# Decay tables doubled on both sides at once, V in bands by way of memory, G's third band from PSUM, v times sums also on GpSimd, a new order

## The chip, the cores and the metric

The kernel runs on one core of a Trainium2 chip. The metric is the device time of one execution in microseconds (us). The engines are PE (TensorE, matmul), DVE (VectorE), ACT (ScalarE), POOL (GpSimd) and SP (SyncE, which here only issues DMAs). Each engine works through its own queue in order and waits for others by semaphores. A change under about 0.2% (0.8 us) can't be told from none here.

## What is computed

```python
# r, k, v: (4, 8, 768, 48);  w, u: (8, 48)
for t in range(S):
    cur = einsum('bhd,bhe->bhde', u * k_t, v_t)
    y_t = einsum('bhd,bhde->bhe', r_t, state + cur)
    state = w * state + einsum('bhd,bhe->bhde', k_t, v_t)
x = y, heads side by side                  # (4, 768, 384)
h = x^T @ U @ V                            # U (768, 32), V (32, 768)
u = x + h^T
out = u + relu(u @ w_ch1) @ w_ch2          # w_ch1 (384, 1536), w_ch2 (1536, 384)
```

## The kernel before

**Attention in chunks.** The 768 steps of a batch are six chunks of 128, each with two halves of 64; a chunk's number n runs over all batches, so 0 to 5 are batch 0. A chunk loads k, r and v (tiles `ld`, `ldk`, `ldr`, `ldv`, L800). PE transposes k and r (L919, into `ptk` and `ptr`). DVE (or ACT and a table on one side) multiplies them by powers of the decay w, from the table `tabT`, into kT and rT (L928; L930 and L931 are copies for chunks that scale k otherwise). PE makes the scores of each half (L951, into `pab`), DVE masks them (L1092, `am`), POOL scales k by the transposed table (L851, L854, `ks`), PE makes the state's updates (L965), DVE adds them to the state S (L1131, L1133), ACT scales S by wm (L1141, `SW`). The diagonal is separate: dv = r * k (L866, POOL), times u (L879), summed per head into dg (L886, DVE), and v * dg, back into `dv` (L890 on ACT per head; L894 on DVE two heads at a time). PE then sums am against v (L988) and S and SW against rT (L992), and DVE adds dv (L1101) to get x.

**The front.** The six chunks of batch 0 come first and nearly alone (the code calls them front(n)). From each x PE makes a part of G = x^T U (L1207, into `wake`). G is split into a high part, a low part and the high part again (L1231, L1239, L1235: three bands of 32 rows in the tile `Gs`), so that one matmul of depth 96 with V in three bands (`V3`: high, high, low) gives x^T U V at full precision. V comes from memory as 128 rows of 192 elements; PE spreads it to three bands of 32 rows by 768 with eight matmuls against the constant `sel` (lines 725 to 740), ACT casts it (L737) and DVE takes the low part (L738). Then PE transposes x and adds V·G into `pu`, `pab` or `pav`, ACT and DVE split the sum into uTh (L1314) and uTl (L1315).

**The MLP.** u goes through w_ch1 and w_ch2 in tiles of 128 by 384 (all these matmuls go through a helper, L473, whose writes are called p). hr is the relu (L1395), hh and hl its high and low parts (L1396, L1397), the last sum is L1435, the store L1443. The weights arrive as 64-bit words (`raw_w`, 384 KB each, L655), are taken apart and joined on DVE and ACT (L677 to L698) and split into high and low parts w1s and w2s (L717, L718). U and V take the same way (`raw_u`, `raw_v`).

**What sets the order.** A planner in the kernel (class Plan) simulates queues, DMAs and PE's instruction fetch (`BLOCK`, `FETCH`, `fetched`) as the program is built, and writes each engine's operations in the order in which they got their turn; each operation has a key, from its place in the code or from the table `RANKS`, which names operations by number. Operations with `alt` go to the engine that would have them done first. Between 10 and 48 us of the planner's time (`PACED`) each DMA that SP issues also waits for an operation of DVE or ACT, so that loads don't run ahead. `at(t, ...)` gives a step its due time; `LATER` is that of V's conversion.

## Time and profile before

| | us |
|---|---|
| timed runs, median of 3 (lowest, highest) | 404.32 (404.26, 404.48) |
| the profiled execution | 405.71 |
| its span | 404.0 |
| PE busy | 391.5 |
| DVE, ACT, POOL busy | 272.9, 186.7, 67.7 |

The span is what the hardware profiler recorded of one execution, from the first instruction to the last. Busy time is without waits; PE's and DVE's idle stretches are what a reader looks for, and which engine or DMA ended each.

### The profile page before, as it was taken

The numbers are of one execution on the slowest core, as the hardware profiler recorded it, in microseconds if no ns is written. First come the engines' busy times: TensorE is split into PE (matmuls) and PEld (weight loads), VectorE is DVE, ScalarE is ACT, GpSimd is POOL, SyncE is SP. The second block draws the span as 40 slices with busy tenths as digits, with TensorE's granted clock in tenths as the row PEclk, the third lists the DMA queues.
The fourth block names the chain that finished last, engine by engine and source line by source line (L and its number), as shares of the span: only waits on it lengthen the run. The fifth ranks groups of instructions, "written<-read, shape, count | busy, mean of one in ns | idle before, by whom it ended". The sixth has DMA issues, their size and how long they took to land.

```text
span 404.0 us, 11959 instructions
## 1 busy us (share of the span) xinstructions
PE 391.5 (97%) x4916; PEld 373.5 (92%) x4916; DVE 272.9 (68%) x618; ACT 186.7 (46%) x451; POOL 67.7 (17%) x83
## 2 busy tenths in 40 slices
PE   8988999999999999999999999999999999999994
PEld 5776998999999999999999999999989999999994
DVE  7988979989988897748944789666855561222122
ACT  3686877789552533421523326322322443323330
POOL 2971001031643321200200123101200000000000
PEclk9999999999999999999999999999999999999999
DMA  9968698985565884675656857754307420001001
GB/s 143 176 156 200 121 265 165 250 239 116 111 129 104 190 175 98 104 130 124 132 75 119 157 118 144 123 89 116 87 3 129 107 60 0 0 2 58 2 0 66
DMA packets 195693, 46.27 MB, mean 115 GB/s; under 512 B 179374, under 2 KB 194096, under 8 KB 195632
## 3 DMA queue, kind: packets, MB, share of 16 engines
q1 hardware_dynamic: 194304, 44.85, 55.2%
q8 instruction: 40, 0.66, 0.6%
q10 hardware_dynamic: 1328, 0.59, 0.5%
q14 instruction: 21, 0.17, 0.1%
HBM read 37.16 MB, written 8.26 MB: 112 GB/s over the span
## 4 chain that ended last, share of the span: by engine, by line
PE 88%; DMA 3%; DVE 3%; ACT 2%; issue 1%; SPq 1%; POOL 0%; DVEq 0%; POOLq 0%
PE p L473 70%; PE pab L951 3%; PE pav L1006 2%; PE pav L1011 2%; DMA raw_w<-in_moe_w_ch_dram 2%; PE pab L965 2%; DMA ld<-in_r_dram 1%; PE pab L473 1%; PE pav L988 1%; PE wake L473 1%; PE pab L1207 1%; PE pav L992 1%; PE ptr L919 1%; PE ptk L919 1%; PE pab L919 1%
## 5 line engine op out<-in xcount | busy, mean ns | idle before, releaser
L473 PE MATMUL p<-uTh,w1s 128*128 128x384 f32 x576 | 148.1, 338 | 0.2 <-ACT hr L1395 0.2
L473 PE MATMUL p<-w2s,hh 128*128 128x384 f32 x576 | 128.8, 336 | 0.6 <-ACT hh L1396 0.6
L1395 ACT ACTIVATE hr<-p 128x384 f32<-128x384 f32 x96 | 47.3, 493 | 156.8 <-PE p L473 152.5
L1397 DVE TENSOR_TENSOR hl<-hr,hh 128x384 fp32r<-128x384 f32 x82 | 45.2, 554 | 89.2 <-ACT hh L1396 76.7
L473 PEld LDWEIGHTS p<-uTh,w1s 128*128 128x128 f32 x576 | 102.5, 188 | 2.0 <-ACT hr L1395 0.7
L473 PEld LDWEIGHTS p<-w2s,hh 128*128 128x128 f32 x576 | 102.0, 188 | 1.4 <-ACT hh L1396 0.9
L473 PE MATMUL p<-uTl,w1s 128*128 128x384 f32 x288 | 96.3, 335 | 0.0
L473 PE MATMUL p<-w2s,hl 128*128 128x384 f32 x288 | 79.2, 339 | 0.0
L473 PEld LDWEIGHTS p<-uTl,w1s 128*128 128x128 f32 x288 | 54.0, 188 | 0.0
L1396 ACT CAST hh<-hr 128x384 fp32r<-128x384 f32 x96 | 49.1, 513 | 9.3 <-PE p L473 7.0
L473 PEld LDWEIGHTS p<-w2s,hl 128*128 128x128 f32 x288 | 52.1, 188 | 0.7 <-DVE hl L1397 0.2
L1397 POOL TENSOR_TENSOR hl<-hr,hh 128x384 fp32r<-128x384 f32 x14 | 14.2, 1014 | 103.9 <-ACT hh L1396 36.2
L890 ACT ACTIVATE dv<-ldv,dg 128x48 f32<-128x48 f32 x92 | 22.1, 321 | 4.2 <-DVE dg L886 3.9
L1435 DVE TENSOR_TENSOR x<-p,x 128x384 f32<-128x384 f32 x33 | 17.3, 547 | 6.8 <-PE p L473 6.7
L1092 DVE TENSOR_TENSOR am<-pab,mask 128x256 f32<-128x256 f32 x48 | 18.8, 412 | 0.2 <-PE pab L951 0.2
L951 PEld LDWEIGHTS pab<-rT,kT 48*64 48x64 f32 x768 | 13.4, 134 | 5.0 <-issue 2.8
L1101 DVE TENSOR_TENSOR x<-pav,dv 128x384 f32<-128x384 f32 x23 | 12.6, 548 | 6.4 <-PE pav L1011 4.8
L951 PE MATMUL pab<-rT,kT 48*64 48x64 f32 x768 | 16.6, 224 | 0.0
L691 DVE SCALAR_TENSOR_TENSOR raw_w<-raw_w 128x384 int32<-128x384 int32 x24 | 13.1, 551 | 0.9 <-POOL w2s L718 0.6
L698 ACT ACTIVATE raw_w<-raw_w 128x384 f32<-128x384 f32 x24 | 13.3, 565 | 0.8 <-DMA raw_w<-in_moe_w_ch_dram 0.8
L886 DVE TENSOR_REDUCE dg<-dv 128x8 f32<-128x384 f32 x24 | 12.9, 540 | 0.1
L910 DVE STREAM_TRANSPOSE kT<-bl 128x256 f32<-128x256 f32 x30 | 12.4, 422 | 0.0
(190 smaller groups left out, 503.0 us busy)
## 6 DMA issues: line engine op xcount, KB each, us to landing
raw_w<-in_moe_w_ch_dram SPq DMA_DIRECT2D x24, 384.0 KB, 5.0
ldv<-in_v_dram SPq DMA_DIRECT2D x24, 192.0 KB, 4.2
ldk<-in_k_dram SPq DMA_DIRECT2D x20, 192.0 KB, 3.5
ldr<-in_r_dram SPq DMA_DIRECT2D x20, 192.0 KB, 3.1
bl<-in_r_dram SPq DMA_DIRECT2D x79, 48.0 KB, 2.7
bl<-in_k_dram SPq DMA_DIRECT2D x79, 48.0 KB, 2.4
ud<-x SPq DMA_DIRECT2D x18, 192.0 KB, 4.2
ub<-ud SPq DMA_DIRECT2D x18, 192.0 KB, 3.6
```

The source lines that it names most:

```text
L473: return nc.tensor.matmul(*args, **kw)
L691: return nc.vector.scalar_tensor_tensor(word(0), word(1), 3, word(0), ALU.logical_shift_left, ALU.bitwise_or)
L698: on_act(n, lambda: nc.scalar.activation(word(1).bitcast(F32), word(1).bitcast(F32), AF.Copy, scale=2.0 ** -112), [(raw, "hi")], loaded)
L886: on_dve(384, lambda e: e.tensor_reduce(dg.t, dv.t, AX.X, ALU.add), [dg], [dv])
L890: nc.scalar.activation(dv.t[:, h], v_of(n, h), AF.Copy, scale=dg.t[:, h:h + 1])
L951: return nc.tensor.matmul(pt.t[o * C2:(o + 1) * C2, q * C2:(q + 1) * C2], lhsT=kT.t[rows, q, i * C2:(i + 1) * C2], rhs=rT.t[rows, q, i * C ...
L1092: on_dve(256, lambda e: e.tensor_tensor(am.t, abs_[n][j].t[:, :SU].rearrange("p (h t) -> p h t", h=NP), mask_.unsqueeze(1).broadcast_to([1 ...
L1101: nc.vector.tensor_tensor(x.t[:, c0:c1], out_bank(n).t[:, c0:c1], dv.t.rearrange("p h d -> p (h d)")[:, c0:c1], ALU.add)
L1395: on_act(384, lambda: nc.scalar.activation(hr.t, pt.t[:, :TB], AF.Relu), [hr], [pt])
L1396: on_act(384, lambda: nc.scalar.copy(hh.t, hr.t), [hh], [hr])
L1397: on_either(384, lambda e: e.tensor_tensor(hl.t, hr.t, f32(hh.t), ALU.subtract), [hl], [hr, hh], only=None)
L1435: on_dve(384, lambda e, x=x, pt=pt: e.tensor_tensor(x.t, pt.t[:, :DM], x.t, ALU.add), [x], [pt])
```

## The change

1. `tables()` builds both sides of the decay table together: the clamped w is written to both, one reciprocal makes the other side, five doublings work on both at once, and the last doubling is done for one table and then for the other. The tile `inv`, two reciprocals, the outer product and two products go.
2. V's three bands are no longer made by PE. The tile `vh` gets the high part (ACT) and the low part (DVE) in the layout of memory, a DMA writes it to `vd` in DRAM, and three DMAs read it back as bands. `sel` and its copy go. `LATER` is 20.05 in place of 30.05.
3. G's third band is copied from PSUM, not from the first band. The rows of G are tracked apart (`G_ROWS`); the last chunk's x comes in two pieces, its product with U in three.
4. v * dg goes in fours of heads, on ACT, DVE or POOL. The first copy of S may go to ACT. Some pads are set by POOL.
5. The planner's constants for PE's instruction fetch are others, and so is the whole table `RANKS`, and with it the order on every engine. The last two stores have exchanged their queues.

```diff
-    BLOCK, FIRST = 126.5, 92
-    FETCH, BUSY, FETCHES = 1400, 1100, 48e3
+    FETCH, BUSY, FETCHES = 1600, 1100, 48e3
+    ASKED = 1500
...
-    sel = wbuf([128, 3 * 128], F32, "xh", NXS, "sel")
+    G_ROWS = [(wk, ("g", g)) for g in range(NCT)]
...
-        on_dve(4, lambda e: e.tensor_scalar(pw[:, 0, :, 1:2], pw_.t[:PD, :NP].unsqueeze(2), W_LO, W_HI, ALU.max, ALU.min),
-               [(tabT, 0)], [pw_])
+        on_dve(8, lambda e: e.tensor_scalar(at_(C2 + 1, (NP * W - 2, 2), (W, NP)),
+                                            pw_.t[:PD, :NP].unsqueeze(1).broadcast_to([PD, 2, NP]), W_LO, W_HI, ALU.max, ALU.min),
+               both, [pw_])
+        on_dve(32, lambda e: e.reciprocal(at_(C2 - 1, (NP * W + 2, 2), (W, NP)), at_(C2 + 1, (NP * W - 2, 2), (W, NP))), both, [])
+        def double(e, m, i, k):
+            o = i * NP * W
+            e.tensor_tensor(at_(o + C2 - 2 * m, (W, k * NP), (3 * m + 1, 2), (1, m)), at_(o + C2 - m, (W, k * NP), (m + 1, 2), (1, m)),
+                            at_(o + C2 - m, (W, k * NP), (2 * m, 2), (0, m)), ALU.mult)
         m = 1
-        while m < C2:
-            on_dve(4 * m, lambda e, m=m: e.tensor_mul(pw[:, 0, :, m + 1:2 * m + 1], pw[:, 0, :, 1:m + 1],
-                                                      pw[:, 0, :, m:m + 1].broadcast_to([PD, NP, m])), [(tabT, 0)], [])
+        while 2 * m < C2:
+            on_dve(16 * m, lambda e, m=m: double(e, m, 0, 2), both, [])
             m *= 2
-        on_dve(100, lambda e: e.reciprocal(inv.t[:, :, 0, 1:], pw[:, 0, :, 1:G8]), [inv], [(tabT, 0)])
-        on_dve(100, lambda e: e.reciprocal(inv.t[:, :, 1, 1:], pw[:, 0, :, G8:C2:G8]), [inv], [(tabT, 0)])
-        on_dve(28, lambda e: e.reciprocal(pw[:, 1, :, C2:], pw[:, 0, :, C2:]), [(tabT, 1)], [(tabT, 0)])
-        on_dve(256, lambda e: e.tensor_mul(pw[:, 1, :, :C2].rearrange("p q (a b) -> p q a b", b=G8),
...
         for x_ in (1, 0):
-            on_dve(256, lambda e, x_=x_: e.tensor_mul(tt[:, x_, :, :C2], pw[:, x_, :, :C2],
-                                                      pw[:, 1 - x_, :, C2:].broadcast_to([PD, NP, C2])),
-                   [(tabT, x_)], [(tabT, 1 - x_)])
+            on_dve(8 * m, lambda e, x_=x_, m=m: double(e, m, x_, 1), [(tabT, x_)], [])
...
         def v_split(fl, raw):
-            def half(j):
-                pt = bank(("tr", "sc")[j], f"pv_{j}")
-                def spread(i, j=j, pt=pt):
-                    c = j * (DM // NV) + i
-                    whole(pt.t[:3 * R, i * NV:(i + 1) * NV],
-                          lhsT=sel.t[:, c * 3 * R:(c + 1) * 3 * R], rhs=fl(),
...
+            vh = wbuf([128, 2, NV], F32R, "xh", NXS, "vh")
+            on_act(NV, lambda: nc.scalar.copy(vh.t[:, 0], fl()), [(vh, 0)], [raw])
+            on_dve(NV, lambda e: e.tensor_tensor(vh.t[:, 1], fl(), f32(vh.t[:, 0]), ALU.subtract), [(vh, 1)], [raw, (vh, 0)], port=True)
+            dma(lambda q: q.dma_start(vd.t.rearrange("i r (c n) -> (r c) i n", n=NV), f32(vh.t)), [vd], [vh], 256, 768, ns=400, late=300)
+            for band, i in enumerate((0, 0, 1)):
+                dma(lambda q, band=band, i=i: q.dma_start(f32(V3.t[band * R:(band + 1) * R]), vd.t[i]), [(V3, band)], [vd], R, 3072, ns=370, late=300)
...
-            for h in range(0, H, 2):
-                op("ACT", 560, lambda h=h: small(h, h + 2), [(dv, h)], vb + [dg], dk=DVK,
-                   alt=[("DVE", dve(2 * D), lambda h=h: nc.vector.tensor_mul(
+            M = 4
+            def wide(e, h):
+                return e.tensor_mul(dv.t[:, h:h + M], vt()[:, h:h + M], dg.t[:, h:h + M].unsqueeze(2).broadcast_to([128, M, D]))
+            for h in range(0, H, M):
+                op("ACT", M * 240 + 80, lambda h=h: small(h, h + M), [(dv, h)], vb + [dg], dk=DVK,
+                   alt=[("DVE", dve(M * D), lambda h=h: wide(nc.vector, h), True), ("POOL", pool(M * D), lambda h=h: wide(nc.gpsimd, h), True)])
...
-        for c0, c1 in ((0, DM),):
+        for c0, c1 in ((0, DM),) if n < NCH - 1 else ((0, 128), (128, DM)):
...
-            on_dve(384, lambda e: e.tensor_copy(new.t, su()), [new], [pst[i]])
+            op("DVE", dve(384), lambda: nc.vector.tensor_copy(new.t, su()), [new], [pst[i]],
+               alt=[("ACT", act(384), lambda: nc.scalar.copy(new.t, su()), False)])
...
             def again_(copy, g):
-                c, _ = piece(g)
-                copy(G.t[2 * R:3 * R, c], f32(G.t[0:R, c]))
+                c, p = piece(g)
+                copy(G.t[2 * R:3 * R, c], p)
...
-                            128 // parts, 1536, ns=375, eng="ACT" if b == B - 1 and t == NTB - 1 and i else "SP")
+                            128 // parts, 1536, ns=375, eng="ACT" if b == B - 1 and t == NTB - 1 and not i else "SP")
...
-    LATER = 30.05
+    LATER = 20.05
```

The order on DVE, from the table's last steps into chunk 1 (kT_1 and rT_1 are chunk 1's, am_0_0 and am_0_1 the two halves of chunk 0's scores, S_0_1 its state after the second half). Before:

```order
L589 TENSOR_TENSOR tabT_83<-inv_93 112x4x64
L593 TENSOR_TENSOR tabT_83<-tabT_83 112x4x64
L928 TENSOR_TENSOR kT_0_167<-ptk_0_134,tabT_83 112x512
L593 TENSOR_TENSOR tabT_83<-tabT_83 112x4x64
L596 TENSOR_TENSOR wm_182<-tabT_83 112x4
L928 TENSOR_TENSOR rT_0_186<-ptr_0_155,tabT_83 112x512
L928 TENSOR_TENSOR kT_1_194<-ptk_1_179,tabT_83 112x512
L928 TENSOR_TENSOR rT_1_219<-ptr_1_196,tabT_83 112x512
L1131 COPY S_0_0_238<-pav1_122 112x384
L1133 TENSOR_TENSOR S_0_1_247<-pst_116,S_0_0_238 112x384
L1092 TENSOR_TENSOR am_0_0_251<-pab0_124,mask_72 128x256
L1092 TENSOR_TENSOR am_0_1_264<-pab1_90,mask_72 128x256
```

And now:

```order
L598 TENSOR_TENSOR tabT_83<-tabT_83 112x8x2x16
L598 TENSOR_TENSOR tabT_83<-tabT_83 112x4x2x32 x2
L606 TENSOR_TENSOR wm_161<-tabT_83 112x4
L934 TENSOR_TENSOR kT_0_163<-ptk_0_130,tabT_83 112x512
L934 TENSOR_TENSOR rT_0_170<-ptr_0_140,tabT_83 112x512
L934 TENSOR_TENSOR kT_1_197<-ptk_1_174,tabT_83 112x512
L1098 TENSOR_TENSOR am_0_0_218<-pab0_95,mask_72 128x256
L1098 TENSOR_TENSOR am_0_1_220<-pab1_113,mask_72 128x256
L934 TENSOR_TENSOR rT_1_233<-ptr_1_222,tabT_83 112x512
L1140 TENSOR_TENSOR S_0_1_244<-pst_107,S_0_0_225 112x384
L934 TENSOR_TENSOR kT_2_264<-ptk_2_235,tabT_83 112x512
```

Both halves of the table now stand ahead of kT of chunk 0, chunk 0's masks have moved ahead of chunk 1's rT and of the state, and the first copy of S has left DVE.

The order on PE at the end of the front and the MLP's start (x_3 to x_5 are the x of chunks 3 to 5, p1_0_0_0 the first MLP tile). Before:

```order
L473 MATMUL pav1_122<-ident_67,x_3_642 128x128
L473 MATMUL pav1_122<-ident_67,x_4_754 128x128
L473 MATMUL p1_0_0_0_889<-uTh_0_0_876,w1s_0_840 128x384 x6
L473 MATMUL p1_0_0_0_889<-uTl_0_0_882,w1s_0_840 128x384 x3
L473 MATMUL pav1_122<-ident_67,x_5_827 128x128
L473 MATMUL pab1_90<-raw_v_522,sel_100 96x192 x2
L473 MATMUL p1_0_0_1_923<-uTh_0_0_876,w1s_1_901 128x384 x2
```

And now:

```order
L485 MATMUL pu0_0_0_828<-V3_780,Gs_0_825 128x384
L485 MATMUL pab0_95<-ident_67,x_3_690 128x128
L485 MATMUL pab0_95<-ident_67,x_4_784 128x128
L485 MATMUL pab0_95<-ident_67,x_5_804 128x128
L485 MATMUL pab0_95<-V3_780,Gs_0_825 128x384
L485 MATMUL pab1_113<-ident_67,x_3_690 128x128
L485 MATMUL pab1_113<-ident_67,x_4_784 128x128
L485 MATMUL pab1_113<-ident_67,x_5_804 128x128
L485 MATMUL pab1_113<-V3_780,Gs_0_825 128x384
L485 MATMUL p1_0_0_0_871<-uTh_0_0_857,w1s_0_814 128x384 x2
```

The spread of V is gone, and two whole sets of transposes with their V·G stand ahead of the first MLP matmul.

The order of SP's DMAs from chunk 4's r on (`bl` are blocks for later chunks, `vsw` v for them). Before:

```order
L800 DMA ldr_4_109<-in_r_dram 128x8x48
L800 DMA ldv_4_373<-in_v_dram 128x8x48
L800 DMA ldv_5_397<-in_v_dram 128x8x48
L800 DMA ldk_5_434<-in_k_dram 128x8x48
L800 DMA ldr_5_114<-in_r_dram 128x8x48
L655 DMA raw_u_485<-in_moe_U_dram 128x6x64
L655 DMA raw_v_522<-in_moe_V_dram 128x384
```

And now, from U's load to the second weight behind V's bands:

```order
L665 DMA raw_u_382<-in_moe_U_dram 128x6x64
L665 DMA raw_v_404<-in_moe_V_dram 128x384
L803 DMA ldk_5_409<-in_k_dram 128x8x48
L803 DMA ldr_5_105<-in_r_dram 128x8x48
L803 DMA ldv_4_473<-in_v_dram 128x8x48
L803 DMA ldv_5_499<-in_v_dram 128x8x48
L665 DMA raw_w1_0_554<-in_moe_w_ch1_dram 128x3x256
L665 DMA raw_w2_0_561<-in_moe_w_ch2_dram 128x768
L821 DMA vsw_6_582<-in_v_dram 64x4x48 x2
L821 DMA vsw_7_626<-in_v_dram 64x4x48 x2
L842 DMA bl_9_0_669<-in_r_dram 32x12x32
L737 DMA vd_675<-vh_631 128x2x192
```

U and V are loaded ahead of chunk 5's k and r and of the last two v, and the write of V's parts (its reads follow after one weight and three blocks) stands behind two weights, four `vsw` and a block.

## Rows read from the trace of the kernel before

**Rows 1.** The page, busy us (share of the span) and instructions of each engine.
```profile
PE 391.5 (97%) x4916; PEld 373.5 (92%) x4916; DVE 272.9 (68%) x618; ACT 186.7 (46%) x451; POOL 67.7 (17%) x83
```

**Rows 2.** Busy us by stage; columns: start:end, length, engines, clock, DMA share, GB/s.
```profile
7.72:42.08 34.36, 30.13 (x754) 25.07 (x754) 30.49 (x71) 23.95 (x79) 19.34 (x23) 1.00 0.95 180
42.08:80.00 37.92, 37.17 (x215) 35.71 (x214) 33.89 (x76) 30.45 (x69) 2.26 (x3) 1.00 0.87 202
50.00:60.00 10.00, 10.00 (x59) 9.97 (x58) 8.57 (x19) 7.83 (x16) 1.03 (x1) 1.00 0.99 265
```
Engines in these rows are PE, PEld, DVE, ACT, POOL.

**Rows 3.** Timeline of DVE, 3.9 to 9: start us, us, engine, line, op, out<-in.
```profile
4.28 0.17 DVE L579 TENSOR_SCALAR tabT<-pab 112x4 f32<-112x4 f32 x1 [0.25 <-PE pab L577]
4.48 1.39 DVE L583 TENSOR_TENSOR tabT<-tabT 112x4 f32<-112x4 f32 x6
...
7.19 0.43 DVE L593 TENSOR_TENSOR tabT<-tabT 112x256 f32<-112x256 f32 x1
7.72 0.69 DVE L928 TENSOR_TENSOR kT<-ptk,tabT 112x512 f32<-112x512 f32 x1
8.33 0.41 DVE L593 TENSOR_TENSOR tabT<-tabT 112x256 f32<-112x256 f32 x1
```

**Rows 4.** Timelines of POOL and of PE: the first ks, and chunk 1's transposes.
```profile
8.94 1.98 POOL L851 TENSOR_TENSOR ks<-ld,tab 128x384 f32<-128x384 f32 x2 [6.95 <-ACT tab L603]
...
9.05 0.66 PE L919 MATMUL ptk<-ident,ld 128*128 128x128 f32 x4
```

**Rows 5.** DVE's groups, 7.72 to 37.72: count, busy us, mean ns, idle before.
```profile
L1101 DVE TENSOR_TENSOR x<-pav,dv 128x384 f32<-128x384 f32 x5 | 2.8, 556 | 1.5 <-PE pav L992 1.1 <-ACT raw_u L698 0.3
...
L894 DVE TENSOR_TENSOR dv<-ldv,dg 128x96 f32<-128x96 f32 x6 | 1.3, 250 | 0.1
L684 DVE SCALAR_TENSOR_TENSOR raw_w<-raw_w 128x384 int32<-128x384 int32 x2 | 1.0, 549 | 0.0
L931 DVE COPY kT<-ptk 112x512 f32<-112x512 f32 x1 | 0.7, 679 | 0.0
L677 DVE TENSOR_SCALAR raw_w<-raw_w 128x384 int32<-128x384 uint8 x2 | 0.6, 352 | 0.0
...
L691 DVE SCALAR_TENSOR_TENSOR raw_v<-raw_v 128x192 int32<-128x192 int32 x1 | 0.3, 346 | 0.0
```

**Rows 6.** Timeline of all engines, 36.9 to 44, rows left out.
```profile
36.93 0.92 PE L473 MATMUL pab<-raw_v,sel 128*96 128x192 f32 x4
37.17 0.55 DVE L1101 TENSOR_TENSOR x<-pst,dv 128x384 f32<-128x384 f32 x1
...
38.98 1.00 DVE L1235 CAST Gs<-Gs 32x128 fp32r<-32x128 f32 x1
...
40.34 0.44 PE L473 MATMUL pu<-V,Gs 96*128 96x384 f32 x1 [0.80 <-DVE Gs L1239]
...
42.08 1.29 PE L473 MATMUL p<-uTh,w1s 128*128 128x384 f32 x6
...
43.84 0.84 PE L473 MATMUL pab<-raw_v,sel 128*96 128x192 f32 x4
```

**Rows 7.** The page, DMA issues: count, KB each, median us to landing.
```profile
ud<-x SPq DMA_DIRECT2D x18, 192.0 KB, 4.2
ub<-ud SPq DMA_DIRECT2D x18, 192.0 KB, 3.6
```

**Rows 8.** Timeline of PE at two stops; the page's row of the instruction queue.
```profile
22.12 0.24 PE L965 MATMUL pav<-ldv,ks 64*48 64x48 f32 x1 [1.29 <-issue]
...
31.70 0.43 PE L988 MATMUL pav<-ldv,am 64*64 64x48 f32 x7 [0.94 <-issue]
...
q8 instruction: 40, 0.66, 0.6%
```

**Rows 9.** The chain of waits near 53 us, and PE's timeline near 65.
```profile
52.76 7.98 DMA raw_w<-in_moe_w_ch_dram
...
64.85 0.96 PE L473 MATMUL p<-w2s,hh 128*128 128x384 f32 x4 [0.59 <-ACT hh L1396]
```

More of the change, by code (lines that the diff above doesn't have):

```diff
@@ L787, in pads @@
             for i in range(2):
[L788 removed]
+                pad = lambda e, i=i: e.memset(part(i)[:, :, D:], 0.0)
+                if n == 0:
+                    on_dve(32, pad, [(t3, f"pad{i}")], [])
+                else:
+                    op("POOL", 250, lambda pad=pad: pad(nc.gpsimd), [(ts[i] if n >= 4 else t3, f"pad{i}")], [])
         if turned(n) and not front(n):
```

51 lines of the change are left out of this document (20 added, 31 removed), and 83 rows, old and new, of the table RANKS.

## The prediction

> **What bounds the kernel now.** I read, in this order, the page's busy times, a table of busy time by stage, and the timeline and the chain of waits of the first 65 us. PE is busy 391.5 of the span's 404.0 us [rows 1], at a granted clock of 1.00 in the stages that matter [rows 2], so the clock is no lever, and a gain has to come from PE work that goes or from the 12.5 us in which PE idles. The stage table says where those lie: 4.2 between 7.72 and 42.08, where the first MLP matmul starts, 0.75 from there to 80 [rows 2]; the other 7.5 lie mostly ahead of the first transposes and behind the last matmul, where the change does little. From 42.08 on PE is fed. Before it, in the front (six attention chunks of batch 0), VectorE is busy 30.5 of 34.4 us [rows 2]: its chain from table to chunk to x sets when the first MLP matmul may start. So the change is worth what it moves that start, plus PE work removed after it, less what is given back later.
>
> The profiled execution took 405.71 us, its span 404.0; the three timed runs have a median of 404.32. I work out differences from the trace and take them off the median.
>
> **1. Tables.** Before, the clamp starts at 4.28, six doublings take 1.39 us from 4.48, then three reciprocals, an outer product and one half (0.43) stand before kT of chunk 0 at 7.72, and the other half (0.41) stands between kT and rT [rows 3]. After: clamp and one reciprocal (0.2 us each by the pitch 4.28 to 4.48), doublings of 16 to 256 elements (the six small ones took 1.39; without the two smallest, 0.17 each, and with one of 0.43, about 1.5), two halves (0.86) and wm (0.16). 4.28 + 0.4 + 1.5 + 0.86 + 0.16 = 7.2: kT starts 0.5 us earlier, rT follows at once, about 1.0 earlier. For VectorE that is worth nothing at once: chunk 1's kT waits for transposes that begin at 9.05, when its k has landed [rows 4], and the first loads keep their order. It is worth something for GpSimd, whose first ks waited 6.95 us for the table and started at 8.94 [rows 4]; from there its sums run without a gap. The halves for table 1 are done at about 6.9 where they were at 7.62, so that chain moves by 0.7 to 1.2.
>
> **2. VectorE's work in the front.** Counted by the order from kT of chunk 0 to x of chunk 5, at durations of [rows 5]: gone are one table half (0.41 [rows 3]), the S copy of chunk 0, now on ACT (384 elements like an x, 0.55), a kT copy, now on ACT (0.68), and three conversion steps that go behind x (0.55 and twice at most 0.35): 2.9. v×dg was 6 pieces of 0.25 and is 5 of twice the width, for which the nearest row is the 128x192 operation of 0.346: +0.23. New are V's low part (0.346) and x of chunk 5 in two pieces (+0.14, a launch more): 0.7. So 2.2 us less work. If VectorE's idle time stayed, x would end 2.2 us earlier than 37.72. It should shrink: its waits are for PE (1.1 ahead of the x alone [rows 5]), and the new order puts chunk 1's and 2's transposes and the scores before the state updates, and GpSimd's chain starts up to 1.2 earlier. Walking the new order row by row with these durations I get x at 34.65, 3.1 earlier. Bounds of this term: 2.2 and 3.1; I take 3.0, near the walk's end, since GpSimd's chain and the scores are what those waits hang on.
>
> **3. From x to the first MLP matmul.** Before: x 37.17 to 37.72, then G's last product, high casts on ACT, then VectorE's second cast of the high part from SBUF, which stood 1.0 us, and lows; the first V·G waited 0.80 for them and the first MLP matmul came at 42.08, 4.36 after x [rows 6]. After: the third band comes from PSUM and waits for no high cast, and the last x goes in two pieces with products of their own. Against that stand two more sets of three transposes and a V·G (about 0.8 of PE work) ahead of the first MLP matmul. My walk gives 3.95: 0.4 less. Zero, if the casts aren't what ends it, is the other bound.
>
> **4. V by memory.** The eight spread matmuls cost PE 0.92 + 0.84 us [rows 6]. The first four lie before the end of x and are hidden there; the other four, at 43.84, are on the path: -0.84. With 3's 0.8, which moves ahead of the first matmul and is in its sum, PE's work after that start falls by 1.6. The new way: cast, subtraction, a write of 196 KB, three reads of 98 KB. No row shows these transfers; the nearest are a write of a similar kind, 4.2 us to landing, and its read back, 3.6 [rows 7]. V's low part is ready at about 28.4, so V3 is there at 28.4 + 4.2 + 3.6 + 0.5 (three issues) = 36.7; G is ready at 36.9 by the walk, 38 by step 5. Cover: 0.2 to 1.3 us. At the front's DMA share of 0.95 [rows 2] each of the two may land later (a weight took 7.98 at a share of 0.99 [rows 9]), and in SP's queue they stand behind weights and states: the cost is 0 to 1.5; I take 0, since 5 delays G too. The selector's copy (ACT, at the start) is hidden before and gone after: 0.
>
> **5. What holds it back: PE's instructions.** PE stood still twice in the front for nothing that the trace shows, 1.29 us before 22.12 and 0.94 before 31.70, in the middle of rows of equal matmuls [rows 8]. The instruction queue brings packets of 16 KB, 40 of them for 4916 matmuls with their weight loads [rows 8]: one per 123 matmuls. Between the two stops lie, by the program's order, 253 passes, two packets, in 9.58 us: 4.8 us a packet when PE has to wait for it. The same number of passes now wants to run some 3 us faster, under the same DMA load (share 0.95 [rows 2]). By that rate the last of these borders, reached at 30.8 before and released at 31.7, is released at 30 to 31, and the first MLP matmul comes at 39.3 to 40.5, not at 42.08 - 3.0 - 0.4 = 38.7. Bounds of this cost: 0 and 1.8; I take 1.1.
> [...]
>
> First MLP matmul: 42.08 - 3.0 - 0.4 + 1.1 = 39.8, 2.3 earlier; PE's work behind it 1.6 less: together 3.9.
>
> **6. What is given back: weights.** Between 42 and 65 the MLP eats weights as they come. The DMA engines' share is 0.99 in 50:60 [rows 2]; the chain of waits runs over one weight transfer of 7.98 us from 52.76, and at 64.85 PE waited 0.59 for ACT's hh [rows 9], which stood behind that weight's conversion. If those weights land when they did, PE waits all 3.9 there. They may come earlier: SP issues loads when VectorE and ACT have done certain operations, which now run 2 to 3 us earlier; but up to that weight the new queue carries five more loads of 192 KB and ten fewer of 48 KB (0.5 MB more, 2.4 us at the 202 GB/s of this stage [rows 2]), and V's 0.5 MB. Conversions moved behind x also land on VectorE, busy 33.9 of 37.9 us here. Bounds: 0 and 3.9; I take 1.5, nearer the first, since the transfers before 50 leave room (0.87 over the stage, against 0.99 within it).
>
> **7. Small edits.** Pads on GpSimd, U and V loads moved ahead of chunk 5's: both are done long before use; 0. The last two stores swap queues, behind the same last x: as much late as early, at most the half microsecond of an issue; I take 0. v×dg of chunk 4 on GpSimd (192 elements, half of an operation of 1.0 us) waits for chunk 4's dg behind the last sum: 0 if dg is early, else up to its own 0.5 on x of chunk 4, inside step 2's bounds. [...]
>
> **Sum:** 404.32 - 3.9 + 1.5 = 401.9.
>
> **Rivals.**
> A. *Everything is kept.* No fetch cost and no give-back: 404.32 - 3.4 - 1.6 = 399.3. For it: SP's loads move with VectorE. Against: two stops in the trace, and the share of 0.99.
> B. *Weights hold the time.* The transfer that landed at 60.74 lands there again; PE arrives earlier and waits longer: 404.3. For it: [rows 9]. Against: the time from 42 to 50, with room.
> C. *Slower: V comes too late.* V3 now hangs on a write and a read that stand in SP's queue behind weights. The first V·G needs it at about 37.9. Each us later costs a us; at 40.3 the gain of 2.4 is used up. If the write is issued at 32.5 instead of 28.5, and both transfers land a us later, V3 is there at 42 and the time is 404.3 + 1.7 = 406.0.
> D. *The change doesn't do what it says:* kT of chunk 0 starts no earlier, if the strided doublings (two rows in one operation) cost more than flat ones. Then step 1 is 0, and that is within the range of step 2: 402.5.
>
> **How the numbers follow.** Forecast (with D) 0.50, own range 400.6 to 403.4; A 0.14; B 0.20; C 0.16. Range 399.6 to 405.2, which leaves out half of A and most of C, 2 in 10. A measurement can tell about 0.2% (0.8 us). Faster by more: 0.48 of the forecast, A, and 0.04 of B: 0.66. Within: 0.02 + 0.14 of B + 0.03 of C: 0.19. Slower: 0.02 of B and 0.13 of C: 0.15.
>
> **What will show it.** Right: kT of chunk 0 at 7.2, GpSimd's first ks at about 7.8; x of chunk 5 ended by 35 to 36; the first MLP matmul at 39.3 to 40.5; stops of PE for nothing shown, of 1 us or more in all, before it; 1 to 2 us of waits for weights, hh or hr between 42 and 70. Wrong: the first V·G waiting for the read of V (C), no wait after 42 (A), a wait of 3 us or more near 62 (B).

## Result and the profile after

The changed kernel takes 408.35 us (median of six runs, 407.76 to 409.99) against 404.71 (404.26 to 405.03) for the kernel before on the same chip: a ratio of 1.0097, interval [1.0077, 1.0118]. A second set of runs gave 409.02 against 404.93, 1.0103 [1.0077, 1.0128]. It is 1% slower; the prediction was 401.9, with 0.66 on faster, and its range ended at 405.2.

The profiled execution of the changed kernel took 409.99 us, its span 408.3. The page's busy times, to be held against [rows 1]:

```profile
PE 392.2 (96%) x4906; PEld 372.2 (91%) x4906; DVE 263.8 (65%) x591; ACT 184.3 (45%) x431; POOL 80.3 (20%) x98
```

VectorE does 9 us less work and GpSimd 12.6 more; PE is busy about as long as before. The busy table by stage, which answers to [rows 2] (from kT of chunk 0 to the first MLP matmul, from there to 80, and 50 to 60):

```profile
7.21:40.70 33.49, 30.54 (x756) 25.59 (x754) 28.77 (x67) 23.34 (x73) 19.88 (x25) 0.98 0.93 189
40.70:80.00 39.30, 37.50 (x368) 35.40 (x368) 31.87 (x71) 29.93 (x62) 7.43 (x9) 0.97 0.92 211
50.00:60.00 10.00, 9.77 (x56) 9.39 (x55) 7.93 (x19) 7.90 (x17) 0.00 (x0) 1.00 0.97 258
```

The first MLP matmul is 1.38 us earlier (40.70 against 42.08), but from there to 80 PE idles 1.80 us, where it idled 0.75. VectorE's timeline shows the front going as the steps said: kT of chunk 0 at 7.21 ([rows 3]: 7.72), and both pieces of chunk 5's x done at 35.07 ([rows 6]: 37.72); then the split of G.

```profile
7.21 0.69 DVE L934 TENSOR_TENSOR kT<-ptk,tabT 112x512 f32<-112x512 f32 x1
...
34.00 0.27 DVE L1107 TENSOR_TENSOR x<-pst,dv 128x128 f32<-128x128 f32 x1
...
34.66 0.41 DVE L1107 TENSOR_TENSOR x<-pst,dv 128x256 f32<-128x256 f32 x1
...
36.31 0.58 DVE L1249 CAST Gs<-wake 32x128 fp32r<-32x128 f32 x2
37.48 0.28 DVE L1253 TENSOR_TENSOR Gs<-wake,Gs 32x128 fp32r<-32x128 f32 x1 [0.59 <-ACT Gs L1245]
38.09 0.60 DVE L1253 TENSOR_TENSOR Gs<-wake,Gs 32x128 fp32r<-32x128 f32 x2 [0.32 <-ACT Gs L1249]
```

PE's timeline at the start of the MLP, the answer to [rows 6]:

```profile
35.47 1.20 PE L485 MATMUL pu<-ident,x 128*128 128x128 f32 x9
37.82 0.44 PE L485 MATMUL pu<-V,Gs 96*128 96x384 f32 x1 [1.15 <-DVE Gs L1253]
...
40.70 0.84 PE L485 MATMUL p<-uTh,w1s 128*128 128x384 f32 x2
41.34 0.84 PE L485 MATMUL pav<-ident,x 128*128 128x128 f32 x3
41.83 0.67 PE L485 MATMUL pav<-V,Gs 96*128 96x384 f32 x1
42.30 0.52 PE L485 MATMUL p<-Gs,V 96*128 96x384 f32 x1
42.62 0.91 PE L485 MATMUL p<-uTh,w1s 128*128 128x384 f32 x4
43.36 0.70 PE L485 MATMUL p<-uTl,w1s 128*128 128x384 f32 x3
43.90 0.51 PE L485 MATMUL p<-Gs,V 96*128 96x384 f32 x2
44.65 0.62 PE L485 MATMUL p<-uTh,w1s 128*128 128x384 f32 x2 [0.23 <-ACT hr L1410]
```

Two things stand here. The first tile is cut in two by a set of transposes and a V·G, so "the first MLP matmul" is no longer the start of an unbroken tile: the first relu starts at 44.10, only 0.19 earlier than before (44.29). And the matmuls are slow: from one 128x384 product's start to the next it is 0.32 us at 40.70 and 0.17 to 0.19 from 42.84 to 43.90. The busy table of this stretch shows why: the granted clock was 0.65, 0.50 and 0.64 in the slices from 39 to 43, after PE had idled 1.15 us ahead of the first V·G, and 1.00 in the slices before and behind.

```profile
36.00:39.00 3.00, 1.68 (x10) 1.06 (x8) 1.97 (x7) 1.05 (x5) 1.01 (x1) 1.00 0.97 245
39.00:40.00 1.00, 1.00 (x7) 0.91 (x7) 0.54 (x2) 0.77 (x3) 0.00 (x0) 0.65 0.54 83
40.00:42.00 2.00, 2.00 (x10) 1.91 (x9) 1.64 (x4) 2.00 (x6) 1.03 (x1) 0.50 0.63 160
42.00:43.00 1.00, 1.00 (x5) 1.00 (x5) 1.00 (x4) 1.00 (x3) 0.00 (x0) 0.64 0.56 146
43.00:44.00 1.00, 1.00 (x8) 1.00 (x7) 1.00 (x3) 0.03 (x1) 0.00 (x0) 1.00 0.76 142
```

A second profiled execution of the changed kernel (after_again, 408.38 us, span 406.6) had a clock of 1.00 there. It gives the cleaner account. All numbers are us; the first relu is from ACT's timeline, PE's end from its last matmul, and idle is the length of the stretch less PE's busy time in it:

| profiled execution | first MLP matmul | first relu | PE's end | PE idle between the last two | span after PE's end |
|---|---|---|---|---|---|
| before | 42.08 | 44.29 | 398.61 | 1.28 | 5.39 |
| after | 40.70 | 44.10 | 400.83 | 3.41 | 7.47 |
| after_again | 40.44 | 43.28 | 399.87 | 3.53 | 6.73 |

So in after_again the first relu is 1.01 us earlier, PE's end 1.26 later, and the span after it 1.34 longer: 2.6 in all, as the two spans have it (406.6 - 404.0). The loss of 2.27 between relu and end shows as idle time: PE's busy time in that stretch is 353.06 against 353.04.

The busy time hides something, though. A matmul's end is modelled 0.33 us after its start although the next can start 0.17 later, so the first 0.16 us of each wait count as busy. Counted from start to start it reads otherwise. Take for each shape of matmul its usual distance to the next one's start (the median over the profiles of this case, 0.173 us for 128x384). From the first MLP matmul to PE's end the matmuls then need 323.4 us, where they needed 324.6, and what lies above that need is 36.0 against 31.95. So 1.2 us of work did go, and 4.1 us of waiting came in its place. Of these, 3.3 are waits for the relu: 3.64 in all, where they were 0.31.

PE's waits in after_again (what waited, for whom, us in total, times, longest):

```profile
PE p L485 <- ACT hr L1410: 2.8, 5, 0.8
...
PE pab L957 <- issue: 1.2, 1, 1.2
PE pu L485 <- DVE Gs L1253: 0.9, 2, 0.7
PE pav L1012 <- issue: 0.4, 1, 0.4
PE p L485 <- ACT hh L1411: 0.3, 1, 0.3
```

In the kernel before, PE's waits for the relu came to 0.2 us. All first products use one PSUM bank, so the first matmul of a tile has to wait until the relu has read the tile before it (below, 108.13 behind a relu that ends at 108.08). In after_again 2, 0, 2, 0 and 0 matmuls stand between a tile's last matmul and the next tile's first at the five places where PE waits (43.84, 48.02, 58.99, 108.13, 117.56). In the kernel before at least five stand at every one of the 95 changes of tile, and the longest wait there is 0.15. PE and ACT at 108, in after_again:

```profile
107.15 0.34 PE L485 MATMUL p<-uTl,w1s 128*128 128x384 f32 x1
108.13 0.61 PE L485 MATMUL p<-uTh,w1s 128*128 128x384 f32 x2 [0.64 <-ACT hr L1410]
```

```profile
107.59 0.49 ACT L1410 ACTIVATE hr<-p 128x384 f32<-128x384 f32 x1 [2.30 <-PE p L485]
```

ACT had nothing else to do here: it had idled 2.30 us and began 0.44 after the start of the tile's last matmul. So these waits come from PE's order, which puts one tile right behind the other.

At the end of the program the last three stores go by other queues: before, the first by SP and the last two by ACT; now the first by ACT and the last two by SP. The last matmul and the last issues, before first and the changed kernel second:

```profile
398.27 0.34 PE L473 MATMUL p<-w2s,hl 128*128 128x384 f32 x1
398.53 0.33 SPq L1443 DMA_DIRECT2D out_dram<-x  x1
399.00 1.31 ACTq L1443 DMA_DIRECT2D out_dram<-x  x2
```

```profile
400.49 0.34 PE L485 MATMUL p<-w2s,hl 128*128 128x384 f32 x1
400.76 0.37 ACTq L1458 DMA_DIRECT2D out_dram<-x  x1
401.22 1.70 SPq L1458 DMA_DIRECT2D out_dram<-x  x2
```

From the last issue's end to the end of the span it is 3.7 us where that issue is on ACT's queue, 5.4 where it is on SP's.

### The profile page after: what moved, and what is told of

Its sections match the earlier page's. It is cut to its first block, busy times and chain, and to the rows that moved or that the text cites. A ratio compares the mean times of both kernels' runs of the same rounds, so it can differ in the third digit from the quotient of the medians.

```text
span 408.3 us, 11914 instructions
## 1 busy us (share of the span) xinstructions
PE 392.2 (96%) x4906; PEld 372.2 (91%) x4906; DVE 263.8 (65%) x591; ACT 184.3 (45%) x431; POOL 80.3 (20%) x98
## 4 chain that ended last, share of the span: by engine, by line
PE 87%; ACT 3%; POOL 3%; DMA 2%; issue 2%; DVE 1%; SPq 0%; DVEq 0%; POOLq 0%; ACTq 0%
PE p L485 74%; PE pab L957 3%; PE pav L1012 2%; PE pav L1017 2%; PE pab L971 2%; PE pab L485 1%; POOL dv L882 1%; DMA raw_w<-in_moe_w_ch_dram 1%; POOL dv L869 1%; DMA ld<-in_r_dram 1%; PE pab L1214 1%; ACT hr L1410 1%; PE pab L925 1%; POOL ks L857 1%; PE wake L485 0%
## 5 line engine op out<-in xcount | busy, mean ns | idle before, releaser
L485 PE MATMUL p<-w2s,hh 128*128 128x384 f32 x576 | 130.5, 337 | 0.3 <-ACT hh L1411 0.3
L1412 DVE TENSOR_TENSOR hl<-hr,hh 128x384 fp32r<-128x384 f32 x76 | 42.2, 556 | 91.3 <-ACT hh L1411 84.4
L1412 POOL TENSOR_TENSOR hl<-hr,hh 128x384 fp32r<-128x384 f32 x20 | 20.3, 1018 | 117.6 <-ACT hh L1411 94.5
L869 POOL TENSOR_TENSOR dv<-ldr,ldk 128x384 f32<-128x384 f32 x10 | 10.2, 1022 | 54.5 <-DVE x L1107 51.4
L882 POOL TENSOR_TENSOR dv<-dv,ub 128x384 f32<-128x384 f32 x14 | 14.2, 1012 | 28.3 <-DVE hl L1412 12.9
L893 ACT ACTIVATE dv<-ldv,dg 128x48 f32<-128x48 f32 x72 | 17.4, 321 | 3.0 <-DVE dg L889 3.0
L1107 DVE TENSOR_TENSOR x<-pav,dv 128x384 f32<-128x384 f32 x23 | 12.6, 549 | 6.8 <-PE pav L1017 6.3
```

The source lines that it names most:

```text
L485: return nc.tensor.matmul(*args, **kw)
L869: o = e.tensor_mul(dv.t, rt()[:, :, :D], kt()[:, :, :D])
L882: on_either(384, lambda e: e.tensor_mul(dv.t, dv.t, ub.t), [dv] + ([pool_done] if n == NCH - 1 else []), [ub], only="POOL" if front(n) els ...
L893: nc.scalar.activation(dv.t[:, h], v_of(n, h), AF.Copy, scale=dg.t[:, h:h + 1])
L1412: on_either(384, lambda e: e.tensor_tensor(hl.t, hr.t, f32(hh.t), ALU.subtract), [hl], [hr, hh], only=None)
```

## Experiments

The theory that they start from: the front gained what was forecast, and three things take more than that back: the tail, the gap ahead of the first V·G with the slow clock behind it, and waits in the MLP. Rivals are named with each. Where several kernels ran on one chip they share the runs of the kernel before.

**The tail.** In the changed kernel the queues of the last three stores are put back (t1), and in the kernel before they are exchanged (t2); the edit of t1:

```diff
-  eng="ACT" if b == B - 1 and t == NTB - 1 and not i else "SP")
+  eng="ACT" if b == B - 1 and t == NTB - 1 and i else "SP")
```

> The changed kernel with the queues of the last three stores put back (first one by SP, the last two by ACT, as before). Theory T (the tail): behind PE's last matmul the changed kernel takes 7.5 us where the kernel before took 5.4, because the last two stores now go out by SP; putting them back gives 2.1 us, so 1.0045 times the kernel before instead of 1.0097, some 406.3 us. Rival (the longer tail is chance of one profile, the loss lies in front and MLP): still 1.0097, 408.3 us.

> The kernel before with the swapped queues alone (first of the last three stores by ACT, the last two by SP). Theory T: 2.1 us slower, 406.8 us, with the stretch behind PE's last matmul at 7.5 us in place of 5.4. Rival: no difference, 404.7.

Measured: t1 407.69, ratio to before 1.0065 [1.0041, 1.0090]; t2 406.19, 1.0021 [1.0002, 1.0040]. In their profiles the span after PE's end is 5.70 (t1) and 6.65 (t2), against 7.47 and 6.73 with the change and 5.39 without. In profiles the exchange costs 1.0 to 2.1 us, in either order, and the two cases don't overlap: 5.4 to 5.8 us behind PE's end in all nine profiles of this case with ACT last, 6.7 to 7.5 in all seven with SP last. In timed runs it is less than theory T's 2.1, at the edge of what can be told: t2 is 1.1 us above its kernel before, with an interval that starts at 1.0002; t1 is 0.7 below the changed kernel's first runs; and between f2 and tf below, which differ by this edit alone, the ratio hardly moved. It is one of the causes, and not the largest.

SP's records tell where the time goes. The last store lands 1.9 to 2.6 us after its issue on either queue. But SP also ends the program: behind its own last issue it loads a flag and branches (0.7 us), its next instruction follows 2.5 to 2.9 us after the branch, and from there to the end of the span it is 1.91 us in every profile. With ACT last, SP does this while the stores are under way, and its next instruction comes within 0.2 us of the last landing. With SP last it comes 0.7 to 1.6 us after it.

**The gap ahead of the first V·G.** PE is kept busy by nine more products of the identity (two matmuls each in the trace) into an unused part of the bank, behind the last transpose (f2), and with the tail put back as well (tf):

```diff
+            for _ in range(9 if (b, t, ct, i) == (0, 0, 2, 2) else 0):
+                o = whole(upt[b, t, ct].t[:, 384:512], lhsT=ident_, rhs=ident_, start=False, stop=False, ...)
```

> The changed kernel with nine small matmuls more (identity by identity, into columns that nothing reads) behind the transposes that stand before the first V times G, where PE idled 1.15 us. Theory C (the clock): PE's granted clock fell to 0.50 from about 39.4 to 42.6 after that idle stretch, and differently from run to run (mean clock 0.991 to 0.998 in the six runs); with the gap filled the clock stays at 1.00, the first MLP matmul comes no later, the time falls by 0.5 to 1.5 us and the runs spread less. Rival (the fall has another cause, such as the slow pace of the whole stretch from 36 to 39, or costs nothing because weights hold the MLP): the clock falls as before, the time stays within 0.3 us of the changed kernel.

> Both edits at once in the changed kernel: queues of the last stores put back, gap filled. If T and C are independent: 2.1 + 0.5 to 1.5 us less, 404.7 to 405.7. What is left over the kernel before then is the loss inside the MLP that the two don't touch.

Measured: f2 408.51, 1.0072 [1.0050, 1.0095]; tf 407.78, 1.0075 [1.0047, 1.0102]. The clock was 1.00 through this stretch in both, and the fills, at 2.17 us, were longer than the gap. The first relu came at 43.96 and 43.64, the waits for the relu rose to 2.9 and 2.8. PE's end, 400.63 and 400.48, is 0.2 to 0.35 earlier than in the first profile of the changed kernel and later than in after_again. So the slow clock cost that execution some time, but it isn't why the kernel is slower: with the clock at 1.00 the loss is still there.

**Tables alone, in the order of before.** The new table operations in the old kernel, whose order stays as it was:

> The kernel before, in its own order on every engine, with the new decay tables alone (clamp and reciprocal for both sides, doublings on both sides; the one half still stands between kT and rT). By the prediction's step 1: kT of chunk 0 at 7.2 in place of 7.72, GpSimd's first ks at 8.0 in place of 8.94, x of chunk 5 earlier by up to 1 us. Rival (VectorE and PE in the front wait for loads and for each other, and PE's work up to the MLP is unchanged, so an earlier table turns into longer waits): x of chunk 5 within 0.3 us of 37.2, time within 0.5 us of the kernel before, ratio 0.999 to 1.001.

> The kernel before with the new tables alone, once more, beside the other two on the same chip. Its first profile had the last tiles 1.8 us ahead of the kernel before, its times (ratio 1.002, 0.999 to 1.005) did not. If the gain is real: again 1 us or more ahead from the first tile on, and a ratio of 0.995 to 0.998. If it was one execution's luck with PE's stops for instructions: ratio 0.999 to 1.002.

Measured: 405.26, 1.0020 [0.9989, 1.0051], and 405.18, 1.0001 [0.9983, 1.0019]: no difference. In the first profile the first MLP matmul came at 40.34, the first relu 1.73 us earlier than before, and PE's end 1.80 earlier: in the old order an earlier start is kept to the end. In the second the start was 42.13 and the clock 0.61 between 40 and 44. The front's length differs that much between executions of one kernel, and the tables' gain is lost in it. The expectation of step 1 was more than met: kT of chunk 0 starts at 6.85 in both profiles, 0.87 earlier than before, and x of chunk 5 ends 1.5 and 1.7 us earlier. So the rival's reason, that x would not move, is wrong; its time is right.

**Without the tables of ranks.** Both kernels with `RANKS = {}`, so that the planner alone sets the order:

> The changed kernel with an empty table RANKS: all of its new operations, in the order that the planner makes without the table. Theory O (the new order is what loses in the MLP: tiles of the first product stand back to back there and PE waits about 0.6 us for hr at each, five times): the sum of waits for hr and hh differs from the 2.6 us of the changed kernel by a microsecond or more, and the time moves with it, in either direction. Rival (the new operations themselves lose, whatever the order): about the time of the changed kernel, 408 us, and more than the kernel before without its table.

> The kernel before with an empty table RANKS. Set against the changed kernel without the table, it tells what the new operations (tables, V by memory, third band, v times sums) are worth when neither order comes from a table. If they are worth what the prediction worked out (front shorter by 2 to 3 us, PE work less by 0.84 at least): the changed operations are 1 to 4 us faster here. If their gain goes into waits: within 1 us of each other. The order from the table in the kernel before should be worth something: this one slower than 404.7.

Measured: the changed kernel 415.54, 1.0233 [1.0205, 1.0261]; the one before 408.13, 1.0071 [1.0046, 1.0097]. The largest of PE's waits in the first:

```profile
PE pu L437 <- DMA V<-vd: 5.5, 1, 5.5
```

Neither expectation holds: the changed operations are 7.4 us slower here, not 1 to 4 faster and not within 1. So the detour of V over memory can cost what rival C feared, 5.5 us here; in the order that goes with the change V isn't waited for at all. What they lose, they lose ahead of the MLP: the first relu comes at 55.65 against 45.16. From there to PE's end it takes 353.75 us, against 355.56 without the table in the kernel before, and against 356.5 to 357.3 for the same operations in the order that goes with the change. So behind the first relu it is the order that loses, and not the operations, in one profile of each (the late start also gave the weights more time).

**The waits in the MLP.** In after_again PE waits for the relu at 43.84 (0.60), 48.02 (0.78), 58.99 (0.23), 108.13 (0.64) and 117.56 (0.58). First, work without use behind the first tile, where the spread of V used to be. The seven products were meant to take 0.8 us; they are 14 matmuls and took 1.48, from 44.17 to 45.65:

> The changed kernel with seven small matmuls more (some 0.8 us of PE work that nothing reads) behind the first MLP tile, where the kernel before had the second half of V's spread and a transpose. The prediction's reading (work there is on the path, so taking the spread away gains 0.84): every later tile 0.8 us later, that is 2.2 + 0.8 = 3.0 us behind the kernel before from tile to tile at the end. Rival K (work there covered a wait: the second tile waits for ACT's hr of the first one, 0.23 us in the changed kernel and about 0.6 where the clock is full, so the spread's time came back as a wait): later tiles come 0.2 to 0.6 later, and the wait for hr before the second tile (44.65 in the changed kernel) is gone.

Measured: 410.94, 1.0135 [1.0089, 1.0180], in two runs.

```profile
44.17 1.72 PE L485 MATMUL p<-ident 128*128 128x128 f32 x14
```

Set matmul against matmul with the first profile of the changed kernel, the first tile's next matmul (at 42.62 in the changed kernel) is 0.13 later, and the second tile's first is 1.17 later. So the wait of 0.23 at the second tile went, and covered 0.4 of the 1.48. The other 1.1 stayed, from tile to tile and past the same waits for the relu, until the changed kernel's profile shows a stop of PE for nothing shown, 0.76 us ahead of 78.81, which this one doesn't have; 0.13 is left behind it. That the stop fell away is luck with the places of PE's stops (last section): 28 more instructions stand ahead of it. So rival K is right for the one wait, and no more than that; the rest of the added work was on the path, as the prediction had it. Then PE's rows are moved at four places (o1): the last third of three tiles ahead of the second products that came first, and the set that cuts the first tile behind it. o2 has that, the tail put back, and four fills in the gap:

```diff
+        N["p1", 0, 0, 1, 2].start = N["p2", 0, 0, 0, 2, 0].start - 0.1
+        N["p1", 0, 1, 7, 2].start = N["p2", 0, 1, 6, 2, 0].start - 0.1
+        N["p1", 0, 1, 9, 2].start = N["p2", 0, 1, 8, 2, 1].start - 0.1
+        for j, k in enumerate([("cx", 0, 1, 2, 0), ("cx", 0, 1, 2, 1), ("cx", 0, 1, 2, 2), ("xu", 0, 1, 2)]):
+            N[k].start = N["p1", 0, 0, 0, 2].start + 0.1 * (j + 1)
```

> The changed kernel with PE's order altered at four places of batch 0's MLP and nowhere else: the last third of tiles 1, 16 and 18 of the first product now goes ahead of the second product's matmuls that stood before it (so that these stand between one tile and the next), and the third set of transposes and V times G goes behind the first tile. Theory O (the changed order puts a tile of the first product right behind the one before it, PE waits for ACT's hr of that one, since both use the same PSUM bank): the waits for hr at 44.65, 48.64, 109.14 and 118.56 (0.23, 0.58, 0.64, 0.58 us) go, later tiles come about 2 us earlier than in the changed kernel, some 0.2 us behind the kernel before at the last tiles instead of 2.2, the time falls to about 406.5. Rival W (weights and ACT's conversions hold the MLP, as the prediction's step 6 had it): the waits move to the next matmuls, and the last tiles stay 1.5 to 2.2 us behind the kernel before.

> The same four places, the queues of the last stores put back, and four small matmuls in the gap before the first V times G (the nine of the earlier run lasted a microsecond longer than the gap). If order, tail and clock are the three parts of the loss: last tiles within 0.7 us of the kernel before, either way, 5.4 to 5.8 us behind PE's last matmul, 404 to 405.5 us, ratio 0.997 to 1.001. If something else is left: still 1 us or more behind.

Measured: o1 408.34, 1.0074 [1.0050, 1.0099]; o2 407.08, 1.0064 [1.0046, 1.0082]. In o1 the waits of theory O became smaller or went where matmuls now stand between two tiles (0.13 at the second tile), but others stand in their place (0.75 for the second tile's relu, 0.41 for hh near 111, 0.42 for the relu near 117), and the time is rival W's. In o2 the tail is as expected, the ratio isn't. In its profile the first relu starts at 42.55, 1.74 us earlier than before, and PE's end is 0.64 later: again 2.4 lost between them. PE still waits 0.76 for the second tile's relu, although nine second products now stand between the tiles. ACT's timeline of o2 shows what stands ahead of this relu, for a tile whose last matmul PE started at 44.61:

```profile
44.35 0.54 ACT L732 CAST w1s<-raw_w 128x384 fp32r<-128x384 f32 x1 [0.51 <-DVE raw_w L708]
44.80 0.54 ACT L732 CAST w2s<-raw_w 128x384 fp32r<-128x384 f32 x1
45.24 0.56 ACT L715 ACTIVATE raw_w<-raw_w 128x384 f32<-128x384 f32 x1
45.83 1.07 ACT L705 CAST raw_w<-raw_w 128x384 f16<-128x384 f32 x1
46.63 0.58 ACT L1424 ACTIVATE hr<-p 128x384 f32<-128x384 f32 x1
```

So a new theory: ACT's order, conversions ahead of relus, is what holds. o3 is o2 with ACT's rows alone moved at three places; o2 and the changed kernel ran beside it:

```diff
+        for f, t, r, h in ((1, 0, 2, 2), (8, 1, 0, 1), (9, 1, 1, 1)):
+            i, j = acts.index(N["hr", 0, t, f]), acts.index(N["hh", 0, t, f])
+            lo = acts[i - r].start if r else N["hr", 0, t, f].start
+            if r:
+                N["hr", 0, t, f].start = lo - 0.2
+            N["hh", 0, t, f].start = lo - 0.1 if r else acts[j - h].start - 0.1
```

> This is o2_all_put_right with ACT's rows moved at three places and the rows of the other engines left as they are: the relu and hh of tile (0,0,1) ahead of two weight conversions, the hh of (0,1,8) ahead of one, the relu and hh of (0,1,9) ahead of one conversion and of SW. (One pair, an uTh cast and an hh of the fifth batch, changes places as well.) In o2 TensorE waited 0.76 us for the relu at 47.27, 0.41 for hh at 110.39 and 0.45 for the relu at 116.36. Theory A, ACT's order is what holds the MLP back: these three waits go, tile (0,0,2) starts about 0.75 us earlier than in o2 and the end comes 1.2 to 1.6 us earlier than o2's, some 405.5 timed, ratio to before about 1.002. Theory B, what the conversions make is itself needed at once: the waits turn up at the second products of the next tile, for w2s or hh, and the end stays within 0.4 us of o2's, about 407, ratio 1.005 to 1.006.

> The same kernel as o2_all_put_right, on this chip beside the other two. Both theories: 406.6 to 407.6, ratio 1.004 to 1.008 to before, with the waits of TensorE for the relu at 47.27 (0.76 us) and 116.36 (0.45) as in its first profile.

> The changed kernel itself, on this chip beside the other two. Ratio to before 1.007 to 1.011, about 408.4; if the tail and the fills are worth what the earlier runs said, o2 is 0.7 to 1.5 us below it.

Measured: o3 408.11, 1.0081 [1.0045, 1.0117]; o2 407.19, 1.0050 [1.0032, 1.0068]; after 409.02, 1.0103. Theory A fell. In o3 a wait of 0.51 for the relu near 117 is left, the wait of 0.76 us for the second relu is gone, and at the second products behind it PE waits for hl, which stands in VectorE's queue behind an operation that waits for the conversion moved back on ACT. PE's timeline and VectorE's, both of o3:

```profile
50.17 0.44 PE L499 MATMUL p<-w2s,hl 128*128 128x384 f32 x1 [0.49 <-DVE hl L1433]
```

```profile
48.85 0.56 DVE L715 SCALAR_TENSOR_TENSOR raw_w<-raw_w 128x384 int32<-128x384 int32 x1 [1.04 <-ACT raw_w L712]
49.44 0.22 DVE L1136 MEMSET pav<- 64x192 f32 x1
49.58 0.53 DVE L1433 TENSOR_TENSOR hl<-hr,hh 128x384 fp32r<-128x384 f32 x1
```

That is theory B, with hl in the place of the w2s that it named first. Over all executions the stretch from the first relu to PE's end reads:

| kernel | first relu | stretch | PE busy | PE idle |
|---|---|---|---|---|
| before | 44.29 | 354.32 | 353.04 | 1.28 |
| b_tab, two executions | 42.56, 44.96 | 354.25, 354.13 | 353.14, 353.19 | 1.11, 0.94 |
| after, after_again | 44.10, 43.28 | 356.73, 356.59 | 353.32, 353.06 | 3.41, 3.53 |
| t1, f2, tf | 45.75, 43.96, 43.64 | 356.85, 356.67, 356.84 | 353.04, 352.71, 352.74 | 3.81, 3.96, 4.10 |
| a1, o1 | 44.51, 42.76 | 356.50, 357.30 | 354.08, 353.91 | 2.42, 3.39 |
| o2, two executions | 42.55, 45.66 | 356.70, 356.89 | 353.46, 353.75 | 3.24, 3.14 |
| o3 | 43.45 | 357.01 | 353.91 | 3.10 |
| without ranks, before and changed | 45.16, 55.65 | 355.56, 353.75 | 353.07, 350.47 | 2.49, 3.28 |

In the new order it is 356.5 to 357.3 in ten executions, whenever the relu started (42.6 to 45.8) and whichever rows were moved; in the old order it is 354.1 to 354.3 (355.5 in t2's profile, where one wait for hh was 1.3 us). The new order costs 2.2 to 3.2 us behind the first relu (1.0 to 1.8 against t2's), and a start that is late or early moves the end by as much. PE's timeline of before shows what the old order had there: behind the first products of the second tile PE did transposes, V·G and Gs·V, 1.04 us of work that ACT was not needed for, while ACT made the next relu (and 0.35 more of it at 48.64, among the second products of the first tile):

```profile
46.35 0.34 PE L473 MATMUL p<-uTl,w1s 128*128 128x384 f32 x1
46.53 0.49 PE L473 MATMUL pab<-ident,x 128*128 128x128 f32 x3
46.78 0.43 PE L473 MATMUL pab<-V,Gs 96*128 96x384 f32 x1
47.04 0.34 PE L473 MATMUL pav<-V,Gs 96*128 96x384 f32 x1
47.22 0.51 PE L473 MATMUL p<-Gs,V 96*128 96x384 f32 x2
47.57 0.88 PE L473 MATMUL p<-w2s,hh 128*128 128x384 f32 x4
```

In the new order this work stands ahead of the first relu. That it was the cover of the waits at 43.84 and 48.02 is read from the two timelines; a1 bears it out for the first of them alone, and a kernel with just this work put back was not tried. The waits at 108 and 117 are of the same kind: no matmul stands between the two tiles. o1 and o3 show that moving a few rows on one engine moves them; no order that avoids all of them was found.

None of these kernels beats the kernel before.

## Why the prediction was wrong

**Steps 1 to 3 held until x.** kT of chunk 0 at 7.21 (forecast 7.2), GpSimd's first ks at 8.02 (about 7.8, before 8.94 [rows 4]), x of chunk 5 done at 35.07 (35 to 36). Step 2's 3.0 measured 2.65 in one execution and 1.98 in the other, where the second piece ran from 35.33 to 35.74. Step 3 failed in size: from x to the first MLP matmul it took 5.63 us with the slow clock (0.50 to 0.65 from 39 to 43) and 4.70 with the full one (1.00), not 3.95. The nine casts and low parts of G, of which step 3 expected a gain, took 2.66 us (36.03 to 38.69) where they took 2.43: ACT and VectorE now both read `wake` and wait for each other in turn, 0.59 and 0.32 us on VectorE's side in the rows above, 0.65 and 0.35 on ACT's. (Why they wait is argued, from the fact that all of them read one bank; a kernel with the third band from SBUF was not run.)

**Step 4 held for V.** The write was issued at 29.0 and landed 2.2 us later, the reads from 31.7 on took 2.8 to 3.7: V was there at about 36.1 (forecast 36.7), ahead of G. Its cost was 0. The other half of this step, "PE's work after that start falls by 1.6", was right in kind and too large: seven matmuls are gone from behind the first MLP matmul (four of the spread, one transpose, two V·G), 1.2 us from start to start. Step 3's 0.8 counted two whole sets as moved, but five of the nine transposes stood ahead of the mark before already. That PE's busy time there does not fall (355.25 before, 355.86 in after_again) is the waiting that counts as busy.

**Step 5 held in what the runs show of it.** One stop for nothing shown is left before the MLP, 1.00 us ahead of 29.76 (forecast: the last border released at 30 to 31), where there were two [rows 8]; the first MLP matmul, 40.44 and 40.70, is at the end of the forecast 39.3 to 40.5. Its size is luck: the same stop, before the same matmul, was 0.26 (o2), 1.16 (after_again), 1.57 (tf) and 1.76 us (o2_again), and one of the two old stops is missing in each profile of the tables alone. The step looked at the front only; in the MLP the new order has a stop of 0.36 us at 77.80 (after_again), where the kernel before has none. After some of these stops the clock was below 1.00 for several us, which no step had: after 1.43 (t1: 0.72 in 30 to 34, 0.50 in 34 to 38) and 1.76 us (o2_again), but not after 1.29 (before: 1.00 up to 42.08 [rows 2]) and 1.57 (tf, mean clock 0.999 over the whole execution). o2_again:

```profile
26.00:30.00 4.00, 2.43 (x74) 2.12 (x71) 3.62 (x8) 3.24 (x13) 2.51 (x3) 1.00 0.62 159
30.00:34.00 4.00, 3.81 (x81) 3.49 (x82) 2.47 (x7) 3.32 (x8) 0.00 (x0) 0.63 0.71 178
34.00:36.00 2.00, 2.00 (x36) 1.91 (x34) 1.24 (x4) 0.85 (x2) 0.00 (x0) 0.50 0.83 191
```

The stops of all profiles stand at borders 256 instructions apart (last section). The page's instruction queue has nearly the same measure: 40 packets, 0.66 MB in all, for 4916 matmuls and as many weight loads, one packet per 246 [rows 1], [rows 8]. That PE stands still for such a packet is the step's reading; no run shows it. "The clock is no lever" was true of the execution read (1.00 [rows 2]), and not of others (0.50 from 40 to 42 in the changed kernel).

**Step 6 is the step that failed: the give-back had the wrong waiter and was too small.** It took 1.5 us, for weights that land late. No wait of PE is for a DMA of weights. Idle time behind the first MLP matmul is 2.29 us longer (3.57 against 1.28), and from start to start the waiting is 4.1 us longer, 3.3 of it for ACT's relu. Its sign of being right, 1 to 2 us of waits for weights, hh or hr between 42 and 70, came true (1.61, all for the relu), but 0.74 of such waits stood in the kernel before too, and as much again follows at 108 and 117. In after_again the relu hardly stands behind conversions: it starts 0.37 to 0.73 us after the start of its tile's last matmul. What the step left out is PE's own order, in which nothing stands between one tile and the next for the time that the relu takes.

**Step 7 missed the tail.** Taken as 0, within half a microsecond, it measured +1.34 and +2.08 in the two profiles; the step saw an exchange of two issues and not SP's work behind its last one. VectorE has no wait for GpSimd's v * dg among its longer ones.

**The sum** against after_again, whose clock was 1.00 in the MLP's first tiles, from start to start: first MLP matmul -1.64 (forecast -2.3), PE's matmuls behind it -1.16 (-1.6), waits and stops behind it +4.06 (+1.5), tail +1.34 (0): +2.6, where the forecast was -2.4. Of the 5.0 us between the two 2.6 are the waits, 1.3 the tail, 0.7 the start, 0.4 the work. Rival B's shape, earlier and waiting longer, is the nearest; what it lacked is that the waits could outgrow the gain, and no rival had the MLP slower than before. (Rival C's own sum has a slip: its delays put V at 42.7, not 42, and the time at 406.7.) Whether the new operations in an order without these waits would beat the kernel before is open.

## What to carry to other kernels

An earlier start is worth something only if the work behind it is still in step: take as the mark the first operation of the chain that sets the pace (here the relu, not the first matmul), and walk the orders of all engines from there. Where two tiles share a buffer, count what stands between them: in the kernel before five matmuls and more covered the relu (longest wait 0.15 us), and in the new order two or none did not (0.23 to 0.78). Work taken from the critical engine gains nothing as far as it covers another engine's latency; ask what that engine does in the meantime before the saving is booked (here 1.2 us of work went and 4.1 us of waiting came). The last stores are worth a look at the end of a kernel: here the engine that also ends the program should not carry the last one (6.7 to 7.5 us behind PE's end with it, 5.4 to 5.8 without).
